# A fused attention, expert and feed-forward kernel on one core: its first attention unit prepared head by head, with half of the stacked copies on GpSimd

## Chip, cores and metric

The kernel runs on one core of a Trainium2 chip. The core has a matrix engine (TensorE, PE in the rows), a vector engine (VectorE, DVE), a scalar engine (ScalarE, ACT), GpSimd (POOL) and an engine that here only issues transfers (SyncE, SP); 16 DMA engines move data. The metric is the device time of one execution in microseconds, the median of several runs.

## What is computed

The reference chains three stages, and the change touches only the first. It is an attention over 2 batches, 8 heads, 768 tokens and head dimension 64 in which a query sees only the keys of its own cluster:

```
q_assign = argmax(normalize(q) . normalize(centroids))     # 16 clusters per head
k_assign = argmax(normalize(k) . normalize(centroids))
scores   = q @ k.T / 8, set to -1e9 where q_assign != k_assign
attn     = softmax(scores);   out = attn @ v
x        = routed experts (top 1 of 8, two gates) of out
y        = (g * sigmoid(1.702 g)) @ w_out  with g = x @ w_in
```

## The kernel before

Attention runs over 8 units, each a batch with a pair of heads; a head has 6 steps of 128 queries, so there are 96 steps. The order of all instructions is written out by hand, and every engine works its own queue in that order; an instruction that waits holds up what stands behind it on its engine.

Preparing a unit means this. The rows of q and k are loaded, transposed on TensorE in threes (`transposes`, L237) and split into a high and a low part: ScalarE writes the high part `Hq` or `Hk` (L240), VectorE the low part `Lq` or `Lk` (L241). `stacks` (L255) copies them by DMA from 64 partitions to 64 others into the operands of the scores: `Q1`, `X` (128 rows) and `Q2`, `Z` (80 rows). `clusters` (L267, L268) multiplies the parts with the centroids in `cblk`, and VectorE adds the products up (L270). The argmax is a maximum (L282), a comparison `eq` (L284 on VectorE for the first unit, L286 and L287 on GpSimd for the others), a product with descending numbers (L288), a second maximum (L295) and a comparison that gives one-hot rows `oh` (L296). The one-hots are transposed (L319 and L303) and land as rows 64 to 79 of `Q2` and `Z`, where they mask the scores: for head 0 of the first unit directly by L322 to L325, else through `ohT` (L305) and DMA (L307, L308).

A step i then takes scores (L379, L380, two matmuls of each), a negated row maximum `nm` (L382, VectorE), the exponential (L388, ScalarE), six transposes of it (L396) whose result is split into `pth` (L400, ScalarE) and `ptl` (L401, VectorE), and the products with v (L418, L419), which begin at loop pass 5.

In PSUM the scores have two buffers, the transposes `pt` two, and one buffer `m` is left over. While the first unit is prepared, `misc` hands out the `m` buffer and the two `pt` buffers in turn (`spots`); after pass 0 of the loop it hands out only `m`. The second unit (u = 1) is prepared during the steps of the first. Its nine pieces are: transposes of q head 0; of q head 1, with the stacks of q; of k head 0; of k head 1, with the stacks of k; clusters q; clusters k and the first half of the argmax; the split of v; the second half of the argmax; the one-hots. `plan_at` says in which pass each is put out; the second half of the argmax goes ahead of its pass's scores. For u = 1 these passes are

```
(0, 0, 0, 1, 3, 4, 7, 6, 7)      # later units: (-3, -2, 0, 1, 3, 4, 7, 6, 7), counted from pass 12 u - 12
```

`keep_clock(n)` issues n matmuls (L130) whose result nobody reads. `setup_centroids` and `setup_blocks` make `cblk`; `setup_rest` fills constants on GpSimd and loads `wo`; `vsplit` (L342, L343) splits v on GpSimd.

Of the kernel before, what the change touches and what calls it, by code (L numbers as in the profile page):

```python
# [9 lines left out]
F32 = mybir.dt.float32  # L10
# [10 lines left out]
C = 16  # L21
# [4 lines left out]
T = S // 128  # L26
# [18 lines left out]
def attention_moe_ffn(ctx: ExitStack, tc: tile.TileContext, q, k, v, centroids, w_gate, w_og, w1, w2, w_in, w_out, out):  # L45
# [69 lines left out]
    def load_unit(u):  # L115
        b, pr = UNITS[u]
        d = st[u] = {}
        for nm, src in (("q", q), ("k", k), ("v", v)):
            t = ld.tile([128, 2, T, D], F32, name=f"ld_{nm}", tag=f"ld_{nm}")
            nc.sync.dma_start(out=t, in_=src[b, 2 * pr:2 * pr + 2].rearrange("h (p t) d -> p h t d", t=T))  # L120
            d[nm] = t
# [10 lines left out]
    def setup_first():  # L132
        nc.vector.memset(idle, 0.0)
        keep_clock(7)
        nc.sync.dma_start(out=craw, in_=centroids.rearrange("h c d -> (h c) d"))
        load_unit(0)
# [12 lines left out]
    def setup_centroids():  # L149
# [15 lines left out]
        nc.vector.tensor_scalar(cnorm[:, 0], craw, cn[:, 6:7], None, op0=ALU.mult)  # L165
        nc.vector.tensor_copy(cnorm[:, 1], cnorm[:, 0])
        nc.vector.tensor_copy(cblk.rearrange("p h a c -> p (h a c)"), zero)
        return cnorm

    def setup_blocks(cnorm):  # L170
        pc = ps_a.tile([128, 512], F32, name="pc", tag="po")
        nc.tensor.transpose(pc[:, :128], cnorm.rearrange("p a d -> p (a d)"), ident)
        for r in range(2):
            src = pc[64 * r:64 * r + 64, :128].rearrange("p (h c) -> p h c", h=H)
            hi = cblk[64 * r:64 * r + 64, :, r, :]
            nc.scalar.copy(hi, src)
            nc.vector.tensor_tensor(cblk[64 * r:64 * r + 64, :, 2 + r, :], src, f32(hi), op=ALU.subtract)
# [39 lines left out]
    def prep_pieces(u):  # L217
# [91 lines left out]

        def first_onehots():  # L310

            flat = d["oh"].rearrange("p t x c -> p (t x c)")
            pts = []
            for x in (0, 2):
                pt = misc(u, "poh")[0:XW].bitcast(BF16)[:, 0:S]
                pts.append(pt[64:80])
# [4 lines left out]
            q2, z = d["Q2"][64:80, 0], d["Z"][64:80, 0]  # L321
            nc.scalar.copy(q2[:, a], pts[0][:, a])  # L322
            nc.vector.tensor_scalar(z[:, a], pts[1][:, a], BIG, -BIG, op0=ALU.mult, op1=ALU.add)
            nc.scalar.activation(z[:, b], pts[1][:, b], AF.Identity, scale=pen_scale[64:80], bias=pen_bias[64:80])
            nc.scalar.copy(q2[:, b], pts[0][:, b])  # L325

        def first_argmax(x0):
            def f():
                if x0 == 0:
                    argmax_b_pad()  # L330
                argmax_a(slice(x0, x0 + 2))
                argmax_b(slice(x0, x0 + 2))
            return f

        def argmax_b_pad():
# [843 lines left out]
```

## Time and profile before

| | us |
|---|---|
| median of 3 runs | 775.97 |
| lowest, highest | 774.4, 778.5 |
| the profiled execution, its own time | 776.47 |
| its span from first to last instruction | 774.6 |

A page of the profile counts the busy time of each engine in the span; a timeline row gives start, duration, engine, line and operation, output and inputs, a count, and in brackets how long the engine had been idle and what released it. All starts are microseconds from the start of the span.

### The profile page before, as it was taken

Reading aid. Unit: us, or ns where it says so; the run is one execution under the profiler, and the core shown is the slowest. Engines: PE = TensorE matmul, PEld = TensorE weight load, DVE = VectorE, ACT = ScalarE, POOL = GpSimd, SP = SyncE. Lnnn points to the kernel's source line nnn. Section 1 sums busy time; section 2 is a strip of 40 time slices with the busy share of each in tenths; the row PEclk is TensorE's granted clock in tenths of the full one; section 3 lists DMA queues with packets and bytes.
Section 4 is the critical chain, followed back from the end, with each engine's and each line's share of the span. In section 5 each row is a group of like instructions: output and inputs, shape, how many; then the busy total and the mean of one; then the engine's idle time right before and its main releaser. Section 6 shows DMA issues by size and latency. Waiting matters only on the chain. (4 is left out here: it accounts for less than half of the span.)

```text
span 774.6 us, 12328 instructions
## 1 busy us (share of the span) xinstructions
PE 739.8 (96%) x4364; PEld 653.5 (84%) x4364; DVE 515.2 (67%) x993; ACT 427.3 (55%) x880; POOL 266.0 (34%) x195
## 2 busy tenths in 40 slices
PE   8999999999999987999999998999999999999996
PEld 5898989899898973999989888977888888888885
DVE  5898898989989873445666677686655567342422
ACT  3686776768677861655667776544534335222221
POOL 4202021120552002666677888543521021110101
PEclk8999999999999996999999999999999999999999
DMA  9854948426260005966566776235631121010101
GB/s 235 190 160 137 247 135 245 126 70 161 69 180 11 1 14 185 314 219 216 173 233 214 254 252 222 71 62 108 78 80 55 54 82 55 0 55 1 55 1 54
DMA packets 65344, 98.23 MB, mean 127 GB/s; under 512 B 8800, under 2 KB 43616, under 8 KB 65280
## 3 DMA queue, kind: packets, MB, share of 16 engines
q1 hardware_dynamic: 62976, 91.12, 40.5%
q0 software_dynamic: 2304, 6.30, 2.2%
q8 instruction: 35, 0.57, 0.3%
q14 instruction: 29, 0.24, 0.1%
HBM read 64.46 MB, written 12.59 MB: 99 GB/s over the span
## 5 line engine op out<-in xcount | busy, mean ns | idle before, releaser
L731 POOL TENSOR_TENSOR w<-raw,w 128x1024 fp32r<-128x1024 f32 x47 | 117.6, 2514 | 29.7 <-ACT w L728 26.9
L401 DVE TENSOR_TENSOR ptl<-pt,pth 128x384 fp32r<-128x384 f32 x192 | 98.1, 548 | 22.3 <-ACT pth L400 21.6
L400 ACT CAST pth<-pt 128x384 fp32r<-128x384 f32 x192 | 83.3, 482 | 45.2 <-PE pt L396 45.1
L1086 DVE TENSOR_TENSOR sg<-ph,sg 128x512 f32<-128x512 f32 x48 | 33.2, 692 | 102.8 <-ACT sg L1085 101.0
L388 ACT ACTIVATE P<-sp,nm 128x768 f32<-128x768 f32 x96 | 87.9, 915 | 13.7 <-DVE nm L382 13.7
L382 DVE TENSOR_REDUCE nm<-sp 128x1 f32<-128x768 f32 x96 | 90.9, 947 | 4.3 <-PE sp L380 4.3
L789 POOL TENSOR_TENSOR w<-csq,w 128x512 fp32r<-128x512 f32 x32 | 43.5, 1359 | 136.8 <-ACT w L788 136.8
L1085 ACT ACTIVATE sg<-ph 128x512 f32<-128x512 f32 x48 | 28.6, 597 | 108.2 <-PE ph L1007 107.5
L396 PE MATMUL pt<-ident,P 128*128 128x128 f32 x576 | 81.3, 275 | 1.4 <-DVE ptl L401 1.2
L1103 PE MATMUL py<-w,gl 128*128 128x512 f32 x192 | 75.3, 392 | 2.4 <-DVE gl L1092 2.4
L1006 PE MATMUL ph<-ytl,w 128*128 128x512 f32 x192 | 76.1, 396 | 0.0
L1005 PE MATMUL ph<-yth,w 128*128 128x512 f32 x192 | 75.9, 395 | 0.0
L1007 PE MATMUL ph<-yth,w 128*128 128x512 f32 x192 | 75.4, 393 | 0.0
L1102 PE MATMUL py<-w,gh 128*128 128x512 f32 x192 | 75.3, 392 | 0.0
L396 PEld LDWEIGHTS pt<-ident,P 128*128 128x128 f32 x576 | 67.3, 140 | 9.2 <-DVE ptl L401 5.8
L1101 PE MATMUL py<-w,gh 128*128 128x512 f32 x192 | 75.0, 390 | 0.0
L379 PE MATMUL sp<-X,Q 128*128 128x384 f32 x192 | 73.4, 382 | 1.3 <-DMA X<-Lk 1.2
L418 PE MATMUL po<-pth,vst 128*128 128x384 f32 x192 | 71.2, 371 | 0.0
L728 ACT CAST w<-raw 128x1024 fp32r<-128x1024 f32 x63 | 65.9, 1045 | 5.7 <-DMA raw<-in_moe_w_dram 5.6
L839 PE MATMUL py<-ht,w 128*128 128x480 f32 (+5 forms) x192 | 61.6, 354 | 5.6 <-DVE room L846 4.7
L380 PE MATMUL sp<-Z,Q 80*128 80x384 f32 x192 | 65.9, 343 | 0.8 <-DMA Z<-Hk 0.5
L419 PE MATMUL po<-ptl,vst 128*128 128x384 f32 x192 | 64.9, 338 | 0.0
(216 smaller groups left out, 1743.8 us busy)
## 6 DMA issues: line engine op xcount, KB each, us to landing
raw<-in_moe_w_dram SPq DMA_DIRECT2D x64, 512.0 KB, 3.6
raw<-in_moe_w_in_dram SPq DMA_DIRECT2D x16, 512.0 KB, 4.8
raw<-in_moe_w_out_dram SPq DMA_DIRECT2D x16, 512.0 KB, 4.2
Q<-Hq SPq DMA_DIRECT2D x32, 192.0 KB, 3.7
xd<-zrow SPq DMA_DIRECT2D x8, 768.0 KB, 5.6
ld_q<-in_q_dram SPq DMA_DIRECT2D x8, 384.0 KB, 3.4
ld_k<-in_k_dram SPq DMA_DIRECT2D x8, 384.0 KB, 3.8
ld_v<-in_v_dram SPq DMA_DIRECT2D x8, 384.0 KB, 4.4
```

Of the source, the lines that this page charges most:

```text
L382: nc.vector.tensor_reduce(nm, sp[:, :, :384], op=ALU.max, axis=AX.XY, negate=True)
L388: nc.scalar.activation(P, L["sp"][:, :, :384], AF.Exp, bias=L["nm"], accum_out=L["sm"][:, j % 3:j % 3 + 1])
L396: nc.tensor.transpose(pt[:, r * 128:(r + 1) * 128], L["P"][:, n, r * 128:(r + 1) * 128], ident)
L400: nc.scalar.copy(hi, src)
L401: nc.vector.tensor_tensor(L["ptl"][:, 3 * n:3 * n + 3, qs], src, f32(hi), op=ALU.subtract)
L731: (eng or nc.gpsimd).tensor_tensor(lo, r, f32(hi), op=ALU.subtract)
L1005: nc.tensor.matmul(ph, wa(key, 0, k, i), yth[:, k, cs], start=(k == 0), stop=False)
L1006: nc.tensor.matmul(ph, wa(key, 0, k, i), ytl[:, k, cs], start=False, stop=False)
L1007: nc.tensor.matmul(ph, wa(key, 1, k, i), yth[:, k, cs], start=False, stop=(k == 3))
L1101: nc.tensor.matmul(po[m], gh[:, ms], wb(key, 0, i), start=first, stop=False)
L1102: nc.tensor.matmul(po[m], gh[:, ms], wb(key, 1, i), start=False, stop=False)
L1103: nc.tensor.matmul(po[m], gl[:, ms], wb(key, 0, i), start=False, stop=last)
```

## The change

The loads of q and k of unit 0 are issued head by head, v after the stacked copies of head 0, and q, k and v of unit 1 later still. Both heads are transposed and split by head (q and k of head 0 first), and clusters, argmax and one-hots of head 0 come before the rest of head 1. Of a head's twelve stacked copies of 64 x 384 numbers, six stay in their partitions and go to GpSimd, and six cross partitions and stay DMAs. Four instructions of head 1's argmax and its one-hots are put out in pass 1 of the loop. The matmuls of `keep_clock` go from 7 and 8 to 5 and 2. The zeroing of `cblk` moves to GpSimd, and the two centroid halves are written by one instruction. For u = 1 the passes of the pieces become (2, 2, 3, 3, 4, 5, 7, 6, 7).

```diff
--- before.py
+++ after.py
@@ -112,13 +112,18 @@
     scatters = []
     zrow = one.tile([128, DM], F32, name="zrow")
 
-    def load_unit(u):
+    def load_unit(u, names="qkv", heads=None):
         b, pr = UNITS[u]
-        d = st[u] = {}
+        d = st.setdefault(u, {})
         for nm, src in (("q", q), ("k", k), ("v", v)):
-            t = ld.tile([128, 2, T, D], F32, name=f"ld_{nm}", tag=f"ld_{nm}")
-            nc.sync.dma_start(out=t, in_=src[b, 2 * pr:2 * pr + 2].rearrange("h (p t) d -> p h t d", t=T))
-            d[nm] = t
+            if nm not in names:
+                continue
+            if nm not in d:
+                d[nm] = ld.tile([128, 2, T, D], F32, name=f"ld_{nm}", tag=f"ld_{nm}")
+            if heads is None:
+                nc.sync.dma_start(out=d[nm], in_=src[b, 2 * pr:2 * pr + 2].rearrange("h (p t) d -> p h t d", t=T))
+            else:
+                nc.sync.dma_start(out=d[nm][:, heads], in_=src[b, 2 * pr + heads].rearrange("(p t) d -> p t d", t=T))
 
     craw = one.tile([128, D], F32, name="craw")
     idle = one.tile([128, 512], BF16, name="idle")
@@ -131,9 +136,11 @@
 
     def setup_first():
         nc.vector.memset(idle, 0.0)
-        keep_clock(7)
+        keep_clock(5)
         nc.sync.dma_start(out=craw, in_=centroids.rearrange("h c d -> (h c) d"))
-        load_unit(0)
+        for h in range(2):
+            load_unit(0, "q", h)
+            load_unit(0, "k", h)
         make_identity(nc, ident)
         nc.vector.tensor_copy(identb, ident)
         ii = one.tile([128, C], I32, name="ii")
@@ -162,19 +169,19 @@
         nc.vector.tensor_scalar(cn[:, 5:6], cn[:, 4:5], 0.5, 1e-6, op0=ALU.mult, op1=ALU.add)
         nc.vector.reciprocal(cn[:, 6:7], cn[:, 5:6])
         cnorm = one.tile([128, 2, D], F32, name="cnorm")
-        nc.vector.tensor_scalar(cnorm[:, 0], craw, cn[:, 6:7], None, op0=ALU.mult)
-        nc.vector.tensor_copy(cnorm[:, 1], cnorm[:, 0])
-        nc.vector.tensor_copy(cblk.rearrange("p h a c -> p (h a c)"), zero)
+        nc.vector.tensor_scalar(cnorm, craw[:, None, :].to_broadcast([128, 2, D]), cn[:, 6:7], None, op0=ALU.mult)
+        nc.gpsimd.tensor_copy(cblk.rearrange("p h a c -> p (h a c)"), zero)
         return cnorm
 
     def setup_blocks(cnorm):
         pc = ps_a.tile([128, 512], F32, name="pc", tag="po")
         nc.tensor.transpose(pc[:, :128], cnorm.rearrange("p a d -> p (a d)"), ident)
+        src = [pc[64 * r:64 * r + 64, :128].rearrange("p (h c) -> p h c", h=H) for r in range(2)]
+        hi = [cblk[64 * r:64 * r + 64, :, r, :] for r in range(2)]
         for r in range(2):
-            src = pc[64 * r:64 * r + 64, :128].rearrange("p (h c) -> p h c", h=H)
-            hi = cblk[64 * r:64 * r + 64, :, r, :]
-            nc.scalar.copy(hi, src)
-            nc.vector.tensor_tensor(cblk[64 * r:64 * r + 64, :, 2 + r, :], src, f32(hi), op=ALU.subtract)
+            nc.scalar.copy(hi[r], src[r])
+        for r in range(2):
+            nc.vector.tensor_tensor(cblk[64 * r:64 * r + 64, :, 2 + r, :], src[r], f32(hi[r]), op=ALU.subtract)
 
     def setup_rest():
 
@@ -307,35 +314,76 @@
                 nc.sync.dma_start(out=f32(d["Q2"][64:80, h]), in_=f32(ot[C * h:C * h + C]))
                 nc.sync.dma_start(out=f32(d["Z"][64:80, h]), in_=f32(ot[32 + C * h:32 + C * h + C]))
 
+        def first_alloc():
+            d["m1"] = one.tile([128, 4, T], F32, name="m1", tag="m1")
+            d["eq"] = one.tile([128, 4, T, C], F32, name="eq", tag="eq")
+            d["m2"] = one.tile([128, 4, T], F32, name="m2", tag="m2")
+            d["oh"] = one.tile([128, T + 1, 4, C], BF16, name="oh", tag="oh")
+            nc.gpsimd.memset(d["oh"], 0.0)
+
+        def first_stacks(h, what):
+
+            def f():
+                for par in range(2):
+                    rows = slice(64 * par, 64 * par + 64)
+                    cs = slice(384 * par, 384 * par + 384)
+                    hi, lo = d["H" + what][rows, h], d["L" + what][rows, h]
+                    if what == "q":
+                        todo = ((d["Q1"][0:64], hi, 0), (d["Q1"][64:128], hi, 1), (d["Q2"][0:64], lo, 0))
+                    else:
+                        todo = ((d["X"][0:64], hi, 0), (d["X"][64:128], lo, 1), (d["Z"][0:64], hi, 0))
+                    for dst, s_, side in todo:
+                        if side == par:
+                            nc.gpsimd.tensor_copy(dst[:, h, cs], f32(s_))
+                        else:
+                            nc.sync.dma_start(out=f32(dst[:, h, cs]), in_=f32(s_))
+            return f
+
+        def first_clusters(h):
+
+            pr = UNITS[u][1]
+            pt = misc(u, "pcl")
+            pv = pt[:, :384].rearrange("p (x t a) -> p x t a", x=2, t=3)
+            w = cblk[:, 2 * pr + h].rearrange("p a c -> p (a c)")
+            for x, nm in enumerate("qk"):
+                for t2 in range(3):
+                    cs = slice(t2 * 128, (t2 + 1) * 128)
+                    nc.tensor.matmul(pv[:, x, t2, :], d["H" + nm][:, h, cs], w, start=True, stop=False)
+                    nc.tensor.matmul(pv[:, x, t2, 0:2 * C], d["L" + nm][:, h, cs], w[:, 0:2 * C], start=False, stop=True)
+            return pt
+
+        def first_argmax(h, pt):
+
+            sc, m1, eq, m2 = (d[nm][:, h::2] for nm in ("sc", "m1", "eq", "m2"))
+            n = [128, 2, T, C]
+            for x in range(2):
+                yield nc.vector.tensor_reduce(
+                    sc[:, x].rearrange("p (t r) c -> p t (r c)", r=2),
+                    pt[:, 192 * x:192 * x + 192].rearrange("p (n a c) -> p n c a", a=2, c=2 * C), op=ALU.add, axis=AX.X)
+            yield nc.vector.tensor_reduce(m1, sc, op=ALU.max, axis=AX.X)
+            yield nc.vector.tensor_tensor(eq, sc, m1[:, :, :, None].to_broadcast(n), op=ALU.is_equal)
+            for x in range(2):
+                yield nc.vector.tensor_tensor(eq[:, x], eq[:, x], rev16[:, None, :].to_broadcast([128, T, C]), op=ALU.mult)
+            yield nc.vector.tensor_reduce(m2, eq, op=ALU.max, axis=AX.X)
+            yield nc.vector.tensor_tensor(
+                d["oh"][:, 1:, h::2].rearrange("p t x c -> p x t c"), eq, m2[:, :, :, None].to_broadcast(n), op=ALU.is_equal)
+
         def first_onehots():
 
             flat = d["oh"].rearrange("p t x c -> p (t x c)")
-            pts = []
-            for x in (0, 2):
+            pts = {}
+            for x in (2, 0):
                 pt = misc(u, "poh")[0:XW].bitcast(BF16)[:, 0:S]
-                pts.append(pt[64:80])
+                pts[x] = pt[64:80]
                 for j in range(T):
                     end = (1 + tile_t(j)) * 4 * C + (x + 1) * C
                     nc.tensor.transpose(pt[:, j * 128:(j + 1) * 128], flat[:, end - XW:end], identb)
             a, b = slice(0, 384), slice(384, S)
             q2, z = d["Q2"][64:80, 0], d["Z"][64:80, 0]
+            nc.vector.tensor_scalar(z[:, a], pts[2][:, a], BIG, -BIG, op0=ALU.mult, op1=ALU.add)
+            nc.scalar.activation(z[:, b], pts[2][:, b], AF.Identity, scale=pen_scale[64:80], bias=pen_bias[64:80])
             nc.scalar.copy(q2[:, a], pts[0][:, a])
-            nc.vector.tensor_scalar(z[:, a], pts[1][:, a], BIG, -BIG, op0=ALU.mult, op1=ALU.add)
-            nc.scalar.activation(z[:, b], pts[1][:, b], AF.Identity, scale=pen_scale[64:80], bias=pen_bias[64:80])
             nc.scalar.copy(q2[:, b], pts[0][:, b])
-
-        def first_argmax(x0):
-            def f():
-                if x0 == 0:
-                    argmax_b_pad()
-                argmax_a(slice(x0, x0 + 2))
-                argmax_b(slice(x0, x0 + 2))
-            return f
-
-        def argmax_b_pad():
-            d["m2"] = one.tile([128, 4, T], F32, name="m2", tag="m2")
-            d["oh"] = one.tile([128, T + 1, 4, C], BF16, name="oh", tag="oh")
-            nc.gpsimd.memset(d["oh"][:, 0], 0.0)
 
         def vsplit():
             hi = d["vst"][:, :, :, 0:D]
@@ -343,10 +391,8 @@
             nc.gpsimd.tensor_tensor(d["vst"][:, :, :, D:2 * D], d["v"], f32(hi), op=ALU.subtract)
 
         if u == 0:
-            return [
-                [transposes("q", 0)], [transposes("q", 1), stacks("q", (0,)), transposes("k", 0), transposes("k", 1), stacks("k"), stacks("q", (1,))],
-                [clusters("q"), first_argmax(0), clusters("k"), first_argmax(2)], [first_onehots], [vsplit], [lambda: onehots((1,))],
-            ]
+            return dict(tr=transposes, stacks=first_stacks, clusters=first_clusters, argmax=first_argmax, alloc=first_alloc,
+                        onehots=first_onehots, vsplit=vsplit, second=lambda: onehots((1,)))
         return [
             [transposes("q", 0)], [transposes("q", 1), stacks("q")], [transposes("k", 0)], [transposes("k", 1), stacks("k")],
             [clusters("q")], [clusters("k"), argmax_a], [vsplit], [argmax_b], [onehots],
@@ -611,7 +657,7 @@
 
     plan_at = {}
     for u in range(1, len(UNITS)):
-        for n, r in enumerate((-3, -2, 0, 1, 3, 4, 7, 6, 7) if u > 1 else (0, 0, 0, 1, 3, 4, 7, 6, 7)):
+        for n, r in enumerate((-3, -2, 0, 1, 3, 4, 7, 6, 7) if u > 1 else (2, 2, 3, 3, 4, 5, 7, 6, 7)):
             plan_at.setdefault((12 * (u - 1) + r, n == 7), []).append((u, n))
     pieces = {}
 
@@ -625,19 +671,38 @@
     with tc.manual_schedule():
         setup_first()
         first = prep_pieces(0)
-        load_unit(1)
         cnorm = setup_centroids()
-        for n, piece in enumerate(first):
-            if n == 1:
-                setup_blocks(cnorm)
-            if n == 3:
-                keep_clock(8)
-            for f in piece:
-                f()
+        first["tr"]("q", 0)()
+        first["alloc"]()
+        first["tr"]("k", 0)()
+        setup_blocks(cnorm)
+        first["stacks"](0, "q")()
+        first["stacks"](0, "k")()
+        load_unit(0, "v")
+        first["tr"]("q", 1)()
+        first["tr"]("k", 1)()
+        sc = [first["clusters"](0)]
+        load_unit(1, "qk")
+        chain = [first["argmax"](0, sc[0])]
+        for _ in chain[0]:
+            pass
+        sc.append(first["clusters"](1))
+        keep_clock(2)
+        chain.append(first["argmax"](1, sc[1]))
+        for _ in range(4):
+            next(chain[1])
+        first["stacks"](1, "q")()
+        first["stacks"](1, "k")()
+        first["onehots"]()
         setup_rest()
+        first["vsplit"]()
+        load_unit(1, "v")
         emit_scores(0)
         emit_exp(0)
         for i in range(NS + 2):
+            if i == 1:
+                for _ in chain[1]:
+                    pass
             nu, r = divmod(i + 3, 12)
             if i == 3 or r == 0 and nu + 2 < len(UNITS):
                 load_unit(nu + 2)
@@ -647,6 +712,8 @@
             tail = i >= NS - TAIL
             if (tail or i % 3 == 2) and ost:
                 ost.popleft()()
+            if i == 1:
+                first["second"]()
             prepare(i)
             if i == 0:
                 spots[:] = [(ps_m, "m")]
```

## Rows read from the trace of the kernel before

**Rows 1.** Busy time by engine in the first seven steps; PEclk is TensorE's granted clock.

```profile
20.96:38.19 17.23, 16.65 (x112) 15.54 (x111) 15.67 (x27) 13.25 (x30) 4.08 (x5) 0.93 0.85 189
```

**Rows 2.** Timeline from the start to the first row maximum.

```profile
4.71 0.20 ACT L158 ACTIVATE cn<-cn 128x1 f32<-128x1 f32 x1
...
5.28 0.49 ACT L240 ACTIVATE Hq<-pqk 128x384 fp32r<-128x384 f32 x1 [0.37 <-PE pqk L237]
...
6.28 0.27 DVE L177 TENSOR_TENSOR cblk<-pc,cblk 64x128 fp32r<-64x128 f32 x1
...
8.01 0.30 PE L267 MATMUL pcl<-cblk,Hq 128*128 128x64 f32 x1 [1.04 <-DVE Lq L241]
...
9.26 0.26 PE L268 MATMUL pcl<-cblk,Lq 128*128 128x32 f32 x1
...
11.08 0.65 DVE L288 TENSOR_TENSOR eq<-eq,rev 128x192 f32<-128x192 f32 x1
...
13.79 0.36 DVE L288 TENSOR_TENSOR eq<-eq,rev 128x192 f32<-128x192 f32 x1
...
14.57 0.36 DVE L296 TENSOR_TENSOR oh<-eq,m 128x192 bf16<-128x192 f32 x1
...
16.46 0.56 DVE L323 TENSOR_SCALAR Z<-poh 16x384 fp32r<-16x384 bf16 x1 [1.53 <-PE poh L319]
...
18.10 0.99 ACT L305 ACTIVATE ohT<-poh,pen_bias,pen_scale 64x768 fp32r<-64x768 bf16 x1
...
20.27 0.66 PE L380 MATMUL sp<-Z,Q 80*128 80x384 f32 x1 [0.46 <-DMA Z<-Hk]
...
20.96 0.96 DVE L382 TENSOR_REDUCE nm<-sp 128x1 f32<-128x768 f32 x1 [3.95 <-PE sp L380]
```

**Rows 3.** Last stacked copy that the first scores need: its issue and time to landing.

```profile
L255 SPq DMA_DIRECT2D Z<-Hk x1: 612/612/612, 14.4 to 14.4; - x1
...
DMA to landing us min/median/max: 5.8/5.8/5.8
```

**Rows 4.** The same for the first stacked copy of unit 1.

```profile
L255 SPq DMA_DIRECT2D Q<-Hq x1: 624/624/624, 24.0 to 24.0; - x1
...
DMA to landing us min/median/max: 2.6/2.6/2.6
```

**Rows 5.** Timeline, copies and casts on GpSimd.

```profile
11.57 0.63 POOL L183 COPY wo<-ident 64x512 f32<-64x512 f32 x1
...
12.53 0.29 POOL L188 CAST ones<-t 128x128 bf16<-128x128 f32 x1
```

**Rows 6.** Timeline of GpSimd and of VectorE, where two instructions overlap.

```profile
69.57 1.83 POOL L343 TENSOR_TENSOR vst<-ld_v,vst 128x768 fp32r<-128x768 f32 x1
...
70.18 1.63 DVE L296 TENSOR_TENSOR oh<-eq,m 128x384 bf16<-128x384 f32 x1
```

**Rows 7.** Timeline, argmax of unit 1 in passes 4 to 6.

```profile
33.22 0.55 DVE L282 TENSOR_REDUCE m<-sc 128x24 f32<-128x384 f32 x1
...
36.06 1.02 POOL L288 TENSOR_TENSOR eq<-eq,rev 128x384 f32<-128x384 f32 x1
...
37.11 0.56 DVE L295 TENSOR_REDUCE m<-eq 128x24 f32<-128x384 f32 x1 [0.49 <-POOL eq L288]
37.70 0.56 DVE L296 TENSOR_TENSOR oh<-eq,m 128x384 bf16<-128x384 f32 x1
38.19 0.94 DVE L382 TENSOR_REDUCE nm<-sp 128x1 f32<-128x768 f32 x1
```

**Rows 8.** Timeline, one set of three transposes of unit 2 in the buffer `m`.

```profile
44.36 0.49 PE L237 MATMUL pqk<-ident,ld_q 128*128 128x128 f32 x3
...
45.84 0.55 DVE L241 SCALAR_TENSOR_TENSOR Lq<-pqk,Hq 128x384 fp32r<-128x384 f32 x1
```

**Rows 9.** Busy time and granted clock of two single microseconds.

```profile
18.00:19.00 1.00, 0.20 (x1) 0.00 (x0) 0.00 (x0) 0.97 (x2) 0.00 (x0) 1.00 1.02 235
...
22.00:23.00 1.00, 1.00 (x6) 0.99 (x5) 0.76 (x1) 1.00 (x3) 0.00 (x0) 0.50 0.44 24
```

## Prediction

> **What bounds the kernel now.** I read the busy time in short windows first, then the timeline of the first 50 us, then the times from issue to landing of single transfers. The start is a chain of waits that ends in the first row maximum at 20.96 us [rows 2]. Head 0's one-hot rows are complete at 14.93 and VectorE has scaled the first half of them by 17.02, but the last score product starts only at 20.27, released by a DMA: VectorE had been idle for 3.95 us [rows 2]. That DMA was issued at 14.4 and needed 5.8 us to land [rows 3], because all stacked copies queue behind the loads of two units; with little in front of it a copy of the same size needs 2.6 us [rows 4]. So before the first step the bound is data arriving. After it, it is three engines in a tight ring: from the first row maximum to the eighth (20.96 to 38.19, 17.23 us) TensorE is busy 16.65 us and VectorE 15.67, which leaves VectorE 1.56 us idle [rows 1]. The steps have no deadline, so what the start gains or these passes lose should travel to the end of the kernel. I therefore make the sum at the eighth row maximum, that of step 7, where both orders have done the same work.
>
> **The start: what is removed and moved.** ScalarE is busy with the centroids until 4.91 [rows 2], so `Hq` of head 0 starts at about 4.95 instead of 5.28 whatever the smaller load brings; the two `keep_clock` matmuls left out ahead of the first transposes, the single instruction for the centroid halves and the zeroing moved to GpSimd lie ahead of that and cost nothing. The load is issued at the same place as before and carries half as much.
>
> VectorE's queue is then `Lq`, `Lk`, two parts of `cblk`, `Lq`, `Lk` of head 1: four at 0.55 [rows 8] and two at 0.27 [rows 2], 2.75 us with hand-overs from 5.5 to about 8.3. The twelve cluster matmuls of head 0 start when `cblk` is complete, about 7.15; twelve took 8.01 to 9.52 [rows 2], so they end at 8.65. The argmax of head 0 is eight instructions of 96 or 192 numbers. I price each like the 192-wide rows, 0.36 [rows 2], too much for the two products of 96, which pays for the hand-overs, and let the first sum overlap the matmuls: 8.65 + 7 x 0.36 = 11.2.
>
> Then the cost of the six plus six copies on GpSimd. Between 128 numbers at 0.29 and 512 at 0.63 [rows 5], 384 come to 0.5 us each: head 0's end at about 8.6 and head 1's run from 8.6 to 11.7, right beside this argmax. A product took 0.65 instead of 0.36 while a GpSimd copy ran [rows 2], and a one-hot comparison that began 0.61 us into a GpSimd instruction of 1.83 took 1.63 us, against 0.56 when alone [rows 6, 7]. The bounds for four such instructions are 0 and 4 x 0.5; I take 0.2 each, nearest to the 0.29 of the copy, so the one-hots are complete at 12.0.
>
> The Trainium skill's page SBUF — State Buffer, section Who interferes with whom, says that a VectorE instruction with two SBUF inputs and a GpSimd instruction that reads SBUF exclude one another until the first one is done. The long comparison agrees with it: it ended 0.41 us after the GpSimd instruction did. By that rule each of the four would wait for a whole copy at worst, and the first row maximum would come some 1.2 us later than in my sum.
>
> Four instructions of head 1's argmax now stand in front of the scaling of the one-hots on VectorE: 4 x 0.38 plus 0.2, so 13.7, and the scaling ends at 14.25 (0.56 [rows 2]). Three matmuls follow; the last took 0.69 until the row maximum could start [rows 2], the two ahead of it at most 0.33 each. The transposes of the one-hots and ScalarE's three copies run meanwhile. First row maximum: 15.5 instead of 20.96, a gain of **5.5 us**. The DMAs: SP issues six copies per head at some 0.6 us [rows 4] from 5.5 on, the last needed one at 8.5. At 2.6 us it lands at 11.1, hidden; at 5.8 us, at 14.3, which is the edge. Load v, the loads of unit 1, head 1's copies and `wo` now stand behind it on SP's queue, and are needed from pass 5 on. Bounds for the gain: 4.3 (every lock paid in full) to 6.5 (none, and full clock).
>
> **The first passes: what is added.** All of it is on VectorE's queue, whose time I count from the first to the eighth row maximum; before it was 15.67 busy and 1.56 idle [rows 1].
>
> Four instructions of head 1's argmax move behind the first steps: 1.3 us, and `ohT`, 0.99 us of ScalarE that ran while all waited for DMA [rows 2], now stands in front of the first copies of the transposed exponential. VectorE waits about 1.2 us for those, and 0.35 for the second scores.
>
> Both transposes of a pair now fall in one pass (2 and 2, 3 and 3), where only the buffer `m` is handed out; before, three sets used three buffers in pass 0. The second set can't start before VectorE has read the first. In such a row the buffer is held from 44.36 to 46.39 [rows 8]. VectorE, done with the first low part, waits for three transposes (0.49 [rows 8]), ScalarE (0.49 [rows 2]) and three hand-overs: 1.25 us, and what it does next, `ptl` and the row maximum of the next step, waits behind it. Two pairs: 2.5 us.
>
> The first half of unit 1's argmax moves from pass 4 to 5, the second stays at the head of pass 6. GpSimd's three instructions end 3.3 us after the maximum they need (33.77 to 37.08 [rows 7]). Before, VectorE had two `ptl` pairs and a row maximum to do meanwhile and waited 0.49; now it has one `ptl` pair of 1.0, so it waits 2.3. The row maximum of step 7 stands behind it.
>
> Sum: 15.67 + 1.3 busy, 0.35 + 1.2 + 2.5 + 2.3 = 6.35 idle: 23.3 us, a loss of **6.1 us**. Bounds: 4.5, if the early idle of 1.55 only replaces the idle of before; 8.3, if `vsplit` (1.83 us on GpSimd [rows 6]), which moves to about 17 us, blocks the moved instructions for 1.5 and the clock costs 0.7.
>
> **How the numbers follow.** The eighth row maximum comes at 15.5 + 23.3 = 38.8 instead of 38.19: 0.6 us later. Made against the profiled execution's 776.47 that is 777.1; this execution lies 0.5 above the median of 775.97, so I predict **776.6**. The two bounds together give 2.0 less to 4.0 more. About 0.5%, 3.9 us, is what a measurement of this kernel can tell from no change; the forecast lies inside it, with a chance of 0.6.
>
> **Rival, faster (0.22).** The waits in passes 2 to 6 are absorbed: TensorE runs scores ahead during them, and the following steps catch up. For it: ScalarE was busy for only 13.25 of the 17.23 us [rows 1], so one of the three has room. Against it: VectorE's 15.67, 91%, leave little to catch up with. If only the added 1.3 us counted, the gain would be 5.5 - 1.3 = 4.2 us: 771.8. It decides where at least 4.5 of the 6.1 us come back.
>
> **Rival, slower (0.18).** TensorE's clock stays at its lower level through passes 0 to 5. It was at 0.50, the 1.2 GHz level, around 22 us, after little work (0.20 us busy of one at 18 us) [rows 9], and the mean of 0.93 to 38.19 [rows 1] shows that it rose soon, while transposes of unit 1 filled passes 0 and 1. Now those have gone, and TensorE waits some 2 us in each of passes 2 and 3. TensorE's 16.65 us in seven steps [rows 1] hold some 1.6 us of scores and exponential transposes a step; at half the clock these take 1.6 more, of which I let half hide behind VectorE: 0.8 us in each of six passes, 4.8 us on top of the 0.6: 781.4. It decides if the lower level lasts past pass 4. The Trainium skill's page TensorE: Matmul & The Clock Gate, Part 1, says that activity releases the clock and idling takes it away, which speaks for this rival.
>
> **Rival, no shift of the start.** The smaller copies still land 5.8 us after issue, and the DMA remains the last wait; then the first row maximum comes at 16 to 16.5 and the time is about 777.5, inside the forecast's own range.
>
> The range takes the bounds of both sums (773.9 to 780.1) and some way to the two rivals: 772.4 to 780.8. Faster 0.22, same 0.6, slower 0.18.
>
> **What would show it.** Right: the first row maximum at 14.5 to 16.5, released by VectorE's or ScalarE's one-hots; VectorE idle over 1 us before the second `Lq` in passes 2 and 3, each released by ScalarE; 2 us or so idle before L295 in pass 6, released by GpSimd; the eighth row maximum within 2 us of 38.19. Wrong: if the row maxima of steps 2 to 7 come 2.4 us apart as before, the gain stays; if the granted clock is 0.50 beyond pass 4, the loss is larger.

## The result, and the profile after

The changed kernel takes 780.42 us (median of 15 runs; 778.52 to 787.3), the kernel before 775.73 (15 runs beside them). The ratio is 1.0063, interval 1.0046 to 1.0081: **4.7 us slower**, where I had forecast no change that a measurement can tell. The time lies inside the range of 772.4 to 780.8, near its upper end, and nearer to the 781.4 of the slower rival than to the 776.6 of the forecast. The profiled execution of the changed kernel has a span of 778.2 us, against 774.6.

The start of the changed kernel, in its timeline from head 0's argmax to the first row maximum (the columns are those of [rows 2]):

```profile
9.57 0.51 POOL L337 CAST Q<-Hq 64x384 fp32r<-64x384 f32 x1
...
9.67 0.61 DVE L364 TENSOR_TENSOR eq<-sc,m 128x192 f32<-128x192 f32 x1
10.32 0.92 DVE L366 TENSOR_TENSOR eq<-eq,rev 128x96 f32<-128x96 f32 x2
...
11.73 0.36 DVE L368 TENSOR_TENSOR oh<-eq,m 128x192 bf16<-128x192 f32 x1
...
13.45 0.56 DVE L383 TENSOR_SCALAR Z<-poh 16x384 fp32r<-16x384 bf16 x1
...
14.04 0.66 ACT L384 ACTIVATE Z<-poh,pen_bias,pen_scale 16x384 fp32r<-16x384 bf16 x1 [6.69 <-DVE Z L383]
...
14.61 0.45 ACT L385 CAST Q<-poh 16x384 fp32r<-16x384 bf16 x1
...
15.16 0.66 PE L426 MATMUL sp<-Z,Q 80*128 80x384 f32 x1 [1.10 <-ACT Q L385]
...
16.50 0.96 DVE L428 TENSOR_REDUCE nm<-sp 128x1 f32<-128x768 f32 x1 [2.50 <-PE sp L426]
```

No DMA ends a wait here any more: the score products wait for ScalarE's copy into `Q2` instead of for the stacked copy of [rows 2], and the first row maximum starts at 16.50 instead of 20.96. So 4.46 us are gained at the start.

They are lost again by the eighth row maximum, which starts at 41.95 instead of 38.19. The stretch between the two maxima, in the windows view that [rows 1] shows of before (start and end, length, busy time of PE, of its weight loads, of DVE, ACT and POOL, each with the number of instructions, then TensorE's granted clock, the DMA engines' busy share and GB/s):

```profile
16.50:41.95 25.45, 20.16 (x118) 18.02 (x117) 17.49 (x30) 14.30 (x31) 6.42 (x7) 0.82 0.71 163
```

It takes 25.45 us instead of 17.23. VectorE is busy 1.82 longer than in [rows 1] and idle 25.45 - 17.49 = 7.96 instead of 1.56. The timeline of VectorE in this stretch shows where the idle time lies; between its rows stand those of the other engines that explain the pairs:

```profile
22.38 1.16 DVE L447 TENSOR_TENSOR ptl<-pt,pth 128x384 fp32r<-128x384 f32 x2 [1.20 <-ACT pth L446]
...
24.33 0.55 DVE L248 SCALAR_TENSOR_TENSOR Lq<-pqk,Hq 128x384 fp32r<-128x384 f32 x1
...
24.93 0.55 PE L244 MATMUL pqk<-ident,ld_q 128*128 128x128 f32 x3 [1.42 <-DVE Lq L248]
...
25.52 0.49 ACT L247 ACTIVATE Hq<-pqk 128x384 fp32r<-128x384 f32 x1 [1.29 <-PE pqk L244]
...
26.04 0.56 DVE L248 SCALAR_TENSOR_TENSOR Lq<-pqk,Hq 128x384 fp32r<-128x384 f32 x1 [1.17 <-ACT Hq L247]
...
30.14 0.56 DVE L248 SCALAR_TENSOR_TENSOR Lk<-pqk,Hk 128x384 fp32r<-128x384 f32 x1 [1.28 <-ACT Hk L247]
...
40.88 0.55 DVE L302 TENSOR_REDUCE m<-eq 128x24 f32<-128x384 f32 x1 [1.84 <-POOL eq L295]
...
41.95 0.95 DVE L428 TENSOR_REDUCE nm<-sp 128x1 f32<-128x768 f32 x1
```

Four waits of VectorE make 5.49 us: for `pth`, ScalarE's first copy of the transposed exponential, which stands behind `ohT`, for the second set of each pair, and for GpSimd's argmax. The rows from 24.33 to 26.04 are one pair: VectorE ends `Lq`, only then may TensorE write the second set into `m`, ScalarE copies it, and VectorE stands still until that is done. The shift of 3.76 us at the eighth row maximum travels on: it is the same at the thirteenth (53.65 against 49.89), and the two spans differ by 3.6. The medians differ by 4.7; what makes up the rest is not settled.

### The profile page after: what moved, and what is told of

The parts are those of the page before. It is cut to its first block, busy times and chain, and to the rows that moved or that the text cites. A ratio compares the mean times of both kernels' runs of the same rounds, so it can differ in the third digit from the quotient of the medians.

```text
span 778.2 us, 12334 instructions
## 1 busy us (share of the span) xinstructions
PE 738.0 (95%) x4355; PEld 653.9 (84%) x4356; DVE 516.3 (66%) x995; ACT 427.4 (55%) x880; POOL 272.7 (35%) x208
## 5 line engine op out<-in xcount | busy, mean ns | idle before, releaser
L1152 ACT ACTIVATE sg<-ph 128x512 f32<-128x512 f32 x48 | 28.6, 597 | 108.2 <-PE ph L1074 107.6
```

## The experiments

After the result I held that the loss comes from the places of unit 1's pieces: two sets of one pass share the buffer `m`, and the argmax of unit 1 has too little in front of it. The rival was that each other place meets another wait. Beside this stood the clock, the instructions of head 1 that were moved into the first steps, and the copies on GpSimd. In every experiment I read the median and the ratio to the kernel before on the same chip, and in the profile the time from the first to the eighth row maximum, because the first alone scatters: it started at 16.50 in the changed kernel and at 17.34 in p_old, whose instructions up to there are the same. The difference is there before the argmax: head 0's first cluster matmuls took 0.27 and 0.26 us in the changed kernel and 0.39 and 0.38 in p_old.

| kernel | median | ratio to before [interval] | first maximum | eighth | between |
|---|---|---|---|---|---|
| before | 775.73 | | 20.96 | 38.19 | 17.23 |
| after | 780.42 | 1.0063 [1.0046, 1.0081] | 16.50 | 41.95 | 25.45 |
| b_plan | 780.78 | 1.0063 [1.0042, 1.0084] | 19.79 | 42.74 | 22.95 |
| p_old | 776.86 | 0.9999 [0.9984, 1.0013] | 17.34 | 39.99 | 22.65 |
| p_gap | 781.81 | 1.0066 [1.0044, 1.0087] | 16.51 | 38.88 | 22.37 |
| p_apart | 782.29 | 1.0075 [1.0055, 1.0095] | 16.58 | 36.24 | 19.66 |
| early | 780.26 | 1.0047 [1.0033, 1.0061] | 17.32 | 42.96 | 25.64 |
| early_old | 773.26 | 0.9968 [0.9955, 0.9982] | 16.56 | 35.19 | 18.63 |
| no_pool | 779.55 | 1.0057 [1.0040, 1.0074] | 16.14 | 41.41 | 25.27 |
| q2_first | 781.17 | 1.0064 [1.0045, 1.0083] | 15.21 | 42.30 | 27.09 |
| filled | 779.02 | 1.0048 [1.0029, 1.0067] | 17.35 | 41.22 | 23.87 |
| best | 772.75 | 0.9958 [0.9945, 0.9972] | 15.79 | 34.57 | 18.78 |
| best_dma | 779.97 | 1.0057 [1.0043, 1.0071] | 15.34 | 41.10 | 25.76 |

In p_gap and p_apart the second half of unit 1's argmax stands behind the eighth row maximum and not ahead of it, so their eighth comes after less work; there the ninth is the one to compare (39.98 in the kernel before, 43.75 in the changed one).

**b_plan: the kernel before with the new passes alone.**

```diff
-        ... (-3, -2, 0, 1, 3, 4, 7, 6, 7) if u > 1 else (0, 0, 0, 1, 3, 4, 7, 6, 7)):
+        ... (-3, -2, 0, 1, 3, 4, 7, 6, 7) if u > 1 else (2, 2, 3, 3, 4, 5, 7, 6, 7)):
```

> The kernel before with only the passes of unit 1's pieces set to the new ones, (2, 2, 3, 3, 4, 5, 7, 6, 7). Theory A: the first row maximum stays at 20.96, waits of 1.2 us appear before the second low part of each pair and of 1.5 to 2 us before the second maximum, the eighth row maximum comes 4.5 to 6 us later than 38.19, and the time is 780 to 782. Rival B: within 2 us of the kernel before.

As theory A expected, the nine numbers alone cost the kernel before as much as the whole change did. In VectorE's timeline of this kernel stand three of the four waits of the changed one, at the same length:

```profile
28.36 0.56 DVE L241 SCALAR_TENSOR_TENSOR Lq<-pqk,Hq 128x384 fp32r<-128x384 f32 x1 [1.16 <-ACT Hq L240]
...
32.34 0.56 DVE L241 SCALAR_TENSOR_TENSOR Lk<-pqk,Hk 128x384 fp32r<-128x384 f32 x1 [1.16 <-ACT Hk L240]
...
41.67 0.55 DVE L295 TENSOR_REDUCE m<-eq 128x24 f32<-128x384 f32 x1 [1.84 <-POOL eq L288]
```

So these waits belong to the passes and not to the new start.

**p_old: the changed kernel with the old passes.** The same line of the changed kernel is put back.

> The changed kernel with the passes of unit 1's pieces put back to (0, 0, 0, 1, 3, 4, 7, 6, 7). Theory A (the new passes cost the time: two sets of transposes in one pass on one PSUM buffer, and a shorter gap for GpSimd's part of the argmax): the first row maximum stays near 16.5 us, the eighth comes 18 to 20 us after it, at 35 to 36.5 instead of 41.95, and the time is 1.5 to 3 us below the kernel before, 773 to 774.5. Rival B (what moved into pass 1, the four argmax instructions and the one-hots of head 1, costs it, or the TensorE clock that is low in any case): the eighth row maximum comes at 40 or later, and the time stays at 778 or more.

It is slower than I expected, and as fast as the kernel before. The gain of the start is eaten here too, mainly by something else. The timeline around pass 1 shows it:

```profile
22.83 0.52 PE L310 MATMUL poh<-identb,oh 128*64 128x128 bf16 x6 [1.76 <-DVE oh L368]
...
23.39 0.99 ACT L312 ACTIVATE ohT<-poh,pen_bias,pen_scale 64x768 fp32r<-64x768 bf16 x1 [1.49 <-PE poh L310]
...
24.43 0.90 PE L244 MATMUL pqk<-ident,ld_k 128*128 128x128 f32 x3 [1.08 <-ACT ohT L312]
...
25.89 0.56 DVE L248 SCALAR_TENSOR_TENSOR Lk<-pqk,Hk 128x384 fp32r<-128x384 f32 x1 [2.25 <-ACT Hk L247]
```

Head 1's one-hots, which the change moved behind step 0, take `m` in pass 1, and the transposes of k, which the old passes place there, wait until `ohT` is read out of it. TensorE's granted clock also fell in this execution, to 0.50 from 24 to 30 us; no run separates its part of the 5.4 us that p_old loses between the two maxima. So the start and the passes are one edit: the moved one-hots need pass 1 free, and what makes room for them makes the pairs in passes 2 and 3.

**p_gap and p_apart: other passes for unit 1.** p_gap moves only the last three pieces back by one pass, to give the argmax more work in front of it; p_apart gives each set of transposes a pass of its own.

```diff
-        ... else (2, 2, 3, 3, 4, 5, 7, 6, 7)):
+        ... else (2, 2, 3, 3, 4, 5, 8, 7, 8)):   (p_gap)
+        ... else (1, 2, 3, 4, 5, 6, 8, 7, 8)):   (p_apart)
```

> The changed kernel with only the second half of unit 1's argmax, the split of v and its one-hots one pass later: (2, 2, 3, 3, 4, 5, 8, 7, 8). Theory A: VectorE's wait of 1.84 us for GpSimd before the second maximum falls below 0.5, and the time is about 1.4 us below the changed kernel, 778.5 to 779.5. Rival B: the wait goes, but another takes its place and the time does not move.

> The changed kernel with unit 1's pieces in passes (1, 2, 3, 4, 5, 6, 8, 7, 8): every set of transposes in a pass of its own, but GpSimd's part of the argmax still has one pass (6 to 7). Theory A: the two waits of 1.17 and 1.28 us before the second low part of a pair disappear, the clock does not fall at 28.5 us, and the time comes 3 to 4 us below the changed kernel, at 776 to 777.5; the wait before the second maximum of the argmax stays, 1 to 2 us. Rival B: no more than 1 us less.

In p_gap the wait of 1.84 is gone, and the ninth row maximum comes 1.74 earlier than in the changed kernel (42.01 against 43.75). But the kernel isn't faster, for the reason that its timeline shows two steps later:

```profile
45.70 0.40 DVE L483 TENSOR_TENSOR xw<-pox,rs 128x240 f32<-128x240 f32 x1
46.15 0.80 PE L310 MATMUL poh<-identb,oh 128*64 128x128 bf16 x6 [2.94 <-DVE xw L483]
...
48.32 1.37 PE L442 MATMUL pt<-ident,P 128*128 128x128 f32 x6
...
49.20 1.01 ACT L446 CAST pth<-pt 128x384 fp32r<-128x384 f32 x2 [1.23 <-PE pt L442]
...
49.72 1.09 DVE L447 TENSOR_TENSOR ptl<-pt,pth 128x384 fp32r<-128x384 f32 x2 [3.62 <-ACT pth L446]
50.72 0.95 DVE L428 TENSOR_REDUCE nm<-sp 128x1 f32<-128x768 f32 x1
```

In pass 8 the output stage's `pox` uses `m` as well. The one-hots of unit 1 wait 2.94 us for it on TensorE. Behind them in TensorE's queue, at a granted clock that fell to 0.50 from 46 to 49 us, stand products with v and the transposes of the exponential; `pth` waits for these on ScalarE, and VectorE loses 3.62: the row maximum at 50.72 comes 2.0 later than the same one in the changed kernel (48.72). p_apart has no pair, and its ninth row maximum comes 1.11 earlier (42.64); but a wait of 2.45 before `Lq` at 23.71 replaced the first pair, the wait for GpSimd stays (1.83), and the same wait of 3.62 follows in pass 8. In both the rival was right: the time didn't fall, because another wait took the place of the one removed.

**early and early_old: head 1's one-hots ahead of the loop.** The rest of head 1's argmax goes right behind head 0's one-hots, and its own one-hots between the first scores and their exponential. early keeps the new passes, early_old takes the old ones as well.

```diff
         first["onehots"]()
+        for _ in chain[1]:
+            pass
...
         emit_scores(0)
+        first["second"]()
         emit_exp(0)
         for i in range(NS + 2):
-            if i == 1:
-                for _ in chain[1]:
-                    pass
...
-            if i == 1:
-                first["second"]()
```

> The changed kernel with the four argmax instructions and the one-hots of head 1 put back ahead of the loop (the instructions right behind the scaling of head 0's one-hots, the one-hots right behind the first scores); unit 1's passes stay (2, 2, 3, 3, 4, 5, 7, 6, 7). Theory A (unit 1's passes alone cost the time): the four instructions fit into the 2.5 us in which VectorE waits for the first scores, the first row maximum stays at 16.5, and less than 1 us is gained, 779.5 to 780.5. Theory C (two costs of like size: the passes, and what moved into pass 1): the third and fourth row maxima come 1.5 to 2.5 us earlier, the waits in passes 2, 3 and 6 stay, and the time is 778 to 779.

> The same with unit 1's passes put back to (0, 0, 0, 1, 3, 4, 7, 6, 7) as well, so that only the order up to the first scores differs from the kernel before. Theory C: no wait over 0.6 us is left on VectorE after the first row maximum, the eighth comes 17 to 18.5 us after the first, at 34 to 35, and the time is 3 to 4.5 us below the kernel before, 771.5 to 773. Theory A: as with the passes alone, 775.5 to 777, because the start's gain of 3.6 to 4.5 us is lost in a place not yet named.

early gains nothing that can be told: the pairs and the argmax wait still stand in it. TensorE was also slow for longer in its profile: score products of 384 columns took 0.52 us up to the one at 29.10 (0.34 from 22.48 on in the changed kernel), and the first pair cost 1.52; how much this hides is open. early_old is faster than the kernel before by 2.5 us, a little less than theory C expected. By the medians, the old passes alone gave 3.6 us against the changed kernel, the early one-hots alone none that can be told, both together 7.2; by the ratios, which compare each with the kernel before on its own chip, the first is 5.0 and the last 7.4. The likely reason is that the two collisions hide each other: while the pairs hold back passes 2 and 3 it doesn't matter when head 1 is ready, and while head 1's one-hots sit in `m` in pass 1 the old passes can't be used.

**no_pool: all stacked copies by DMA.** The test `side == par` is dropped, so that the twelve copies of GpSimd go to SP's queue.

> The changed kernel with all twelve stacked copies of each head as DMAs and none on GpSimd. If the GpSimd copies hold up the argmax by sharing a port with VectorE, the first argmax's comparison (0.61 us) and two products (0.92 us together) shrink to 0.36 and about 0.55 and head 0's one-hots are complete 0.6 us earlier, at 11.5; if the DMAs are what the copies on GpSimd spare, the first score product waits for a DMA instead, and the first row maximum comes 1 to 3 us later than 16.5, 17.5 to 19.5. I expect the second to decide, and a time 1 to 2 us above the changed kernel.

I had thought that a late DMA would then decide. It didn't: the first maximum starts at 16.14, 0.36 earlier than in the changed kernel, which is within its scatter. VectorE's timeline prices the copies beside the argmax:

```profile
10.09 0.36 DVE L362 TENSOR_TENSOR eq<-sc,m 128x192 f32<-128x192 f32 x1
10.49 0.43 DVE L364 TENSOR_TENSOR eq<-eq,rev 128x96 f32<-128x96 f32 x2
...
11.41 0.36 DVE L366 TENSOR_TENSOR oh<-eq,m 128x192 bf16<-128x192 f32 x1
```

Against 0.61, 0.92 and 0.36 in the changed kernel that is 0.74 us for the four instructions.

**q2_first: ScalarE's copies ahead of the scaling.** The one-hots of q are transposed first, and the two copies into `Q2` stand ahead of the scaling of `Z`.

```diff
-            for x in (2, 0):
+            for x in (0, 2):
...
+            nc.scalar.copy(q2[:, a], pts[0][:, a])
+            nc.scalar.copy(q2[:, b], pts[0][:, b])
             nc.vector.tensor_scalar(z[:, a], pts[2][:, a], BIG, -BIG, op0=ALU.mult, op1=ALU.add)
             nc.scalar.activation(z[:, b], pts[2][:, b], AF.Identity, scale=pen_scale[64:80], bias=pen_bias[64:80])
-            nc.scalar.copy(q2[:, a], pts[0][:, a])
-            nc.scalar.copy(q2[:, b], pts[0][:, b])
```

> The changed kernel with the one-hots of q transposed first and ScalarE's two copies into Q2 issued ahead of the scaling of Z. The prediction had ScalarE's three copies run beside VectorE's work; in the changed kernel they stand behind the scaling that ends at 14.01. If that order cost the missing microsecond of the start, the two copies run from 12.9 to 13.9, the first score product of Z and Q2 starts at 14.0 to 14.7 instead of 15.16, and the first row maximum comes at 15.6 to 16.1. If not, it stays within 0.2 of 16.5. The time changes by less than 1 us either way.

The first maximum came at 15.21, 1.3 us earlier, but the time did not fall. In the timeline, ScalarE's copies and the score product are where they were meant to be, and VectorE and GpSimd show the next collision:

```profile
12.54 0.47 ACT L383 CAST Q<-poh 16x384 fp32r<-16x384 bf16 x1 [5.24 <-PE poh L380]
...
13.77 0.66 ACT L386 ACTIVATE Z<-poh,pen_bias,pen_scale 16x384 fp32r<-16x384 bf16 x1 [0.39 <-DVE Z L385]
...
13.88 0.66 PE L426 MATMUL sp<-Z,Q 80*128 80x384 f32 x1 [0.31 <-DVE Z L385]
...
17.28 1.82 POOL L391 TENSOR_TENSOR vst<-ld_v,vst 128x768 fp32r<-128x768 f32 x1
17.37 2.01 DVE L366 TENSOR_TENSOR eq<-eq,rev 128x96 f32<-128x96 f32 x2
```

Two products of 96 numbers take 2.01 instead of the 0.57 that they took at this place in the changed kernel, because they now begin beside `vsplit` and end 0.28 us after it. The Trainium skill's page SBUF — State Buffer, section Who interferes with whom, calls this an exclusive lock; these two rows agree. In the changed kernel the products begin at 18.66, when `vsplit` (17.14 to 18.95) is nearly over; the time at which they come is what spares them. These 1.44 us take back most of the gain: the third row maximum comes at 20.08, against 20.22. Of what follows a part is the clock, which stood at 0.50 here until 28.6 us: the first pair's wait is 1.52 instead of 1.17.

**filled: TensorE kept busy in the pairs.** In passes 2 and 3, six matmuls whose result nobody reads are put ahead of the second set.

```diff
+                if u == 1 and h == 1:
+                    z = ps_a.tile([128, 512], F32, name="zz", tag="po")
+                    for _ in range(6):
+                        nc.tensor.matmul(z, idle[:, 0:128], idle, start=True, stop=True)
```

> The changed kernel with six matmuls that nobody reads (128x512, into the PSUM buffer of the products with v, free until pass 5) ahead of the second set of transposes in passes 2 and 3, where TensorE waits some 2 us. If the clock, which fell to 0.50 from 28.5 to 33 us, takes part of the loss, it stays at 1.00 there, the fifth to the seventh row maxima come 1 to 1.5 us earlier, and the time is 778.5 to 779.7; the waits for the buffer stay. If it takes nothing, the time stays at 780 to 781.

The windows of the changed kernel from 27 us, then two of no_pool, and two rows of the timeline of filled around the same step:

```profile
27.00:28.00 1.00, 0.20 (x2) 0.00 (x0) 1.00 (x3) 1.00 (x3) 0.00 (x0) 1.00 0.62 144
28.00:29.00 1.00, 0.09 (x1) 0.09 (x2) 0.86 (x2) 0.03 (x1) 0.00 (x0) 1.00 0.93 210
...
30.00:31.00 1.00, 1.00 (x7) 1.00 (x6) 0.79 (x2) 0.69 (x3) 0.00 (x0) 0.50 1.03 296
31.00:32.00 1.00, 1.00 (x5) 1.00 (x4) 0.89 (x2) 1.00 (x2) 0.00 (x0) 0.50 0.99 215
```

```profile
29.00:30.00 1.00, 0.12 (x1) 0.12 (x2) 0.83 (x2) 0.01 (x1) 0.00 (x0) 1.00 0.89 312
30.00:31.00 1.00, 1.00 (x10) 1.00 (x11) 0.01 (x1) 0.53 (x2) 0.00 (x0) 1.00 0.76 197
```

```profile
28.23 0.95 DVE L432 TENSOR_REDUCE nm<-sp 128x1 f32<-128x768 f32 x1
...
32.21 0.95 DVE L432 TENSOR_REDUCE nm<-sp 128x1 f32<-128x768 f32 x1
```

In the changed kernel TensorE was busy 0.20 and 0.09 in two successive microseconds, and its granted clock then stood at 0.50, the 1.2 GHz level, from 30 to 32 us. From the fifth to the sixth row maximum it needed 4.74 us (27.44 to 32.18) and to the seventh 3.38 (35.56). In filled these are 3.98 and 2.60; the waits of 1.16 in the pairs and of 1.83 for GpSimd stay. b_plan and no_pool, which have the same pairs and kept 1.00 there without the six matmuls, show 3.98 and 2.60 as well, and p_gap, whose clock fell too, 4.88 and 3.24. So this fall costs 1.5 us, and the pairs cost without it as well. That the six matmuls are what prevented it isn't shown: in no_pool TensorE was busy 0.17 and 0.12 in two successive microseconds (28 to 30), and the clock stayed. The fifth row maximum of filled came 0.79 later than in the changed kernel, not earlier as expected, because its first came 0.85 later; the eighth came 0.73 earlier. The medians of the two kernels differ by 1.4, but their intervals overlap; it is the profile that separates them.

The changed kernel's granted clock was low once before, at 0.50 from 9 to 22 us, so through its first three row maxima. No run prices this. The windows of filled show 1.00 there, but its score products took 0.52 to 0.53 us up to the one at 20.52, just as the changed kernel's do at 0.50 (later ones take 0.34), so that it was slow there too; from the first row maximum to the fifth it needed 10.88 us, the changed kernel 10.94.

**best and best_dma.** best joins early_old and q2_first; best_dma is best with all stacked copies by DMA.

> The kernel with the old passes and head 1's argmax and one-hots ahead of the loop (773.3 us), and also the two copies into Q2 issued ahead of the scaling of Z. The four argmax instructions then lie before GpSimd's long instruction of vsplit (17.3 to 19.1 us), which had taken back the 1.3 us of this order when it stood alone. If that lock is what took them back, the first row maximum comes at 15.2 to 15.6 instead of 16.56, the shift stays to the eighth, near 34, and the time is 1 us lower, 771.5 to 772.8. If something else, as the copies of head 1 that unit 1 waits for, holds the next steps, the eighth stays at 35.2 and the time at 773.3.

> The same with all stacked copies of the first unit as DMAs. Unit 1 writes its high and low parts into the buffers that head 1's stacked copies read; with twelve DMAs per head, head 1's are issued from 15 us on instead of from 10.8, and land after 20. If those buffers decide, ScalarE waits for a DMA before the first high part of unit 1, 1.5 to 4 us, and the time is 1 to 4 us above the run with GpSimd copies. If not, it is the same or up to 0.5 us lower, since the argmax loses its lock.

best takes 772.75 us, 3.0 less than the kernel before it on its chip and 7.7 less than the changed kernel; it is the fastest here, though not to be told from early_old, so that the order of q2_first is not shown to gain anything here. VectorE's timeline has, up to the eighth maximum, no wait over 1 us but one of 1.41 before the second:

```profile
18.15 0.96 DVE L428 TENSOR_REDUCE nm<-sp 128x1 f32<-128x768 f32 x1 [1.41 <-PE sp L426]
...
33.49 0.55 DVE L302 TENSOR_REDUCE m<-eq 128x24 f32<-128x384 f32 x1 [0.51 <-POOL eq L295]
34.08 0.56 DVE L303 TENSOR_TENSOR oh<-eq,m 128x384 bf16<-128x384 f32 x1
34.57 0.94 DVE L428 TENSOR_REDUCE nm<-sp 128x1 f32<-128x768 f32 x1
```

Without GpSimd's copies the same kernel loses all of it: best_dma takes 7.2 us more than best, where I had expected 1 to 4. ScalarE's timeline in best_dma:

```profile
21.67 0.87 ACT L247 ACTIVATE Hq<-pqk 128x384 fp32r<-128x384 f32 x2 [3.69 <-DMA Q<-Lq]
25.69 0.49 ACT L247 ACTIVATE Hk<-pqk 128x384 fp32r<-128x384 f32 x1 [3.14 <-DMA Z<-Hk]
```

The copies of unit 0 read from `Hq`, `Lq`, `Hk` and `Lk`, and unit 1 may write these buffers only when the DMAs have landed. The first scores don't need GpSimd's half (15.34 against 15.79), but the old passes do, because they overwrite the sources early. This is why no_pool, whose passes come later, lost nothing by it.

## Why the prediction was right or wrong

**The start** was right in its mechanism and 1.0 us too large (4.46 instead of 5.5). The one-hots of head 0 are complete at 12.09, where I had 12.0, and the price of 0.2 us for each of four instructions beside GpSimd's copies came out at 0.74 in all (no_pool). The scaling on VectorE ends at 14.01 (14.25). The step that failed is "The transposes of the one-hots and ScalarE's three copies run meanwhile": ScalarE begins its half of `Z` only when VectorE's is done, at 14.04, and the copy into `Q2` stands behind it in order, so that the score product starts 1.15 us after the scaling. The trace of the kernel before had already shown this order of the two halves, behind the 16.46 to 17.02 of VectorE in [rows 2]:

```profile
17.05 0.66 ACT L324 ACTIVATE Z<-poh,pen_bias,pen_scale 16x384 fp32r<-16x384 bf16 x1 [0.76 <-DVE Z L323]
```

q2_first turned the copies round and had its first maximum at 15.21, 0.3 from my 15.5. The rival of a start that doesn't shift, held up by the DMA, fell: no DMA ends VectorE's or TensorE's wait there, not even with twelve more of them. Its number for the first maximum, 16 to 16.5, came all the same, by luck.

**The loss in the passes** was 8.2 instead of 6.1. Its places were right. The wait behind `ohT` is 1.20 (1.2 predicted), the pairs 1.17 and 1.28 (1.25 each), the wait for GpSimd 1.84 (2.3), the argmax moved behind the first step 1.28 busy (1.3). With the 0.46 that VectorE waits for ScalarE just ahead of it, the wait for GpSimd is the 2.3 of the sum, and the second scores cost 0.32 (0.35). What the sum put at nothing are four further waits of 0.21 to 0.57, together 1.35 us, gaps too small for the rows to name, 0.34, and 0.52 more of busy time than the 16.97 that I had: these are the missing 2.1 us, less 0.1 that the pairs and the second scores saved. One cause of them is TensorE's clock between the fifth and the seventh row maximum, worth 1.5 us by the runs that kept it; a part of that is also in the 1.28 of the second pair. So the rival with the low clock was right in part: the clock was low through the first three row maxima, at a price that no run shows, it rose, and it fell again after the fifth, which cost 1.5 where the rival had 4.8 for six passes. In filled, without this second fall, the stretch is 23.87, 0.6 above my 23.3. The bound of 8.3 that I had given for a low clock and a blocked argmax was nearly reached, though `vsplit` blocked next to nothing in the changed kernel: the two products beside it took 0.57, against 0.43 for head 0's in no_pool.

**The sum** was made of two large terms of opposite sign, and each was off by 1 to 2 us to the same side: 0.6 was forecast at the eighth row maximum and 3.76 came. The range held because it was wide; the forecast of no change that can be told did not. The rival that the waits are absorbed fell. VectorE catches nothing up: the 3.76 at the eighth maximum is there at the thirteenth.

**Where the gain went** is settled as far as this: the new passes alone cost the kernel before as much as the whole change does (b_plan, the same ratio of 1.0063), and the new start with the old passes gains nothing, since head 1's late one-hots collide in `m` (p_old); with both out of the way it gains 2.5 us (early_old). How the 8.2 us divide between the pairs, the argmax wait and `ohT` is not, because the parts don't add up: b_plan loses 5.7 us between the two maxima and p_old 5.4, together more than both at once. The granted clock was low at other times in each of these profiles, and only its second fall in the changed kernel has a price.

## What to carry to other kernels

Work moved off an idle start lands in a steady state where every engine is nearly full; price it there, wait by wait, and list every user of a shared buffer in each pass before giving a pass to a further one. Test such edits alone and together: here two of them were worth 3.6 us and nothing that can be told alone, and 7.2 together (by the medians). When a forecast is the difference of two large terms, its error is that of the terms, not that of the difference.

## What was not expected of the hardware

ScalarE's half of `Z` and VectorE's half are different columns of one tile and read the same PSUM buffer, and yet ScalarE waited until VectorE's instruction had ended (13.45 to 14.01, then 14.04); the kernel before had the same order. It isn't the tile as a whole that orders them, since in q2_first the score product over VectorE's half of `Z` started at 13.88 while ScalarE was writing the other half (13.77 to 14.43). That leaves the shared buffer, which no run tests by itself. VectorE's products beside GpSimd instructions that read SBUF paid from 0.25 us each (beside copies of 0.50) to 1.4 for two (beside `vsplit`). TensorE's clock fell in the changed kernel after rows with 0.20 and 0.09 busy. The Trainium skill's page TensorE: Matmul & The Clock Gate, Part 1, says that idling takes the clock away. In this kernel a wait for a buffer can be enough for that, but it need not be: in no_pool, with 0.17 and 0.12, the clock stayed at 1.00.
